# VectorE's part of a softmax: groups of four heads of one tile, with contiguous passes, in the last five full-width stretches

## The chip, the core and the metric

One core of one Trainium2 chip runs the whole program. The time is what the device takes from the start of the program to its end, in microseconds (us). The median of three runs of the kernel before is 804.98 us (804.66 to 805.05).

The core has a matrix engine (TensorE; PE in the profile, PEld its weight loads), a vector engine (VectorE, DVE), an engine for functions such as the exponential (ScalarE, ACT), a general engine (GpSimd, POOL) and SyncE (SP), which issues transfers. Matrix products land in PSUM, eight banks of 2 KB for each of 128 partitions. Everything else is kept in SBUF.

## What is computed

Two attention layers over the same 2048 x 512 input, 32 heads of width 16, mixed by a gate that is one number for each row:

```python
g = sigmoid((x * gate_w).sum(-1))
# A: full attention
scores = einsum("bhqd,bhkd->bhqk", q, k) * 16 ** -0.5
a = (softmax(scores) @ v) @ A_wo
# B: each position looks back at 8 positions, 2 apart, with a masked softmax
b = (softmax(local logits) @ v) @ B_wo
out = g * a + (1 - g) * b
```

The work is in A: 32 heads x 2048 x 2048 scores, each of which needs an exponential.

## The kernel before

**Blocks and periods.** A's scores are handled in blocks: 128 keys (a tile) x 512 queries of one head. A period is one group of 4 heads with one quarter of the queries: 16 tiles x 4 heads = 64 blocks. There are 8 groups and 4 quarters, so 32 periods; the last is cut into two halves of 256 queries, in which one block holds two tiles. The code counts periods 0 to 32, of which 31 and 32 are the halves, with 32 blocks each.

**Two ways to the exponential.** Most blocks are ScalarE's. TensorE writes the scores of three blocks, then of two, then of three, into two rings of PSUM banks (3 + 2 banks, `ring`), and ScalarE takes each set in one instruction (128 x 1536 or 128 x 1024 elements, line 1420) and writes `pT`. TensorE then multiplies `pT` with the values (`vp_all`, line 1278) into an accumulator, four heads at a time in four column strips of the array.

The others are VectorE's; `n_dve` (line 20) says how many in each period. For each such block, TensorE writes the scores into a bank `misc_ps` (`dq`, line 1332), and VectorE turns them in one instruction into 16-bit integers that read as bf16 are a coarse exponential (`p1`, line 1338, into a group's buffer `dt`). A group has `NGR` = 3 blocks. When its three are there, VectorE makes three further copies of the group, each with another constant added (`sh`, line 1357, into `pd_a`; one "pass" each), and TensorE multiplies the original and the three copies with four differently weighted copies of the values (`vp_all`, and `vd_all` for the passes; `pv` and `dpv`, lines 1367 and 1373). Their sum evens out the error of the coarse form. A group thus costs TensorE four rounds, in each of which its heads run side by side.

**Two forms of a pass.** Up to period `FLAT0` = 28 a pass is written with rows of 514 elements (`ROW`) and read in half rows (line 1361). From period 28 on it is one contiguous stretch of 3 x 512 elements on both sides (line 1363). [...]

**Buffers.** Groups from period 8 on take turns in three `dt` buffers: `dt_a` and two in `wkv`, weights that are no longer needed by then (line 507). Passes take turns in three `pd_a` buffers. PSUM has three banks besides the rings, shared by the accumulators (at most two) and by every `misc_ps`.

**B.** The local attention runs mostly on GpSimd, tile by tile, 16 tiles of 43 us; its projections use the weights `bw`. When GpSimd has made the rows of a tile (`obb`), TensorE transposes them and VectorE copies them (`fin` and `oe`, lines 1210 and 1217). GpSimd also scales A's finished accumulators (`po2a`, `po2b`, lines 1462 and 1465) except in the last three periods, where VectorE does.

**Order.** No engine chooses its order when it runs. Every piece of work is an `op` with its engine, a cost, a due time, what it depends on and which buffers it takes. `list_schedule` (line 181) walks through time and picks for each engine the piece that is next; what comes out is written to each engine's queue as it stands, and each engine works through its own in order, waiting where an input or a buffer is not ready. `sets` and `beside` (lines 447 to 471) decide beside which of ScalarE's sets a VectorE block's scores are written: at most one to a set, and by preference one of a head that the set does not have. `p1` has a due time 100 us ahead of need (`P1D`, line 123), so that it goes before the passes.

Of the kernel before, what the change touches and what calls it, by code (L numbers as in the profile page):

```python
# [9 lines left out]
ALU = mybir.AluOpType  # L10
AX = mybir.AxisListType
FP32 = mybir.dt.float32
BF16 = mybir.dt.bfloat16
# [3 lines left out]

CFG = dict(
    set_sizes=(3, 2),
    n_dve=(3, 3, 6, 6, 9, 9, 12, 12) + (12,) * 20 + (15,) + (15,) * 2 + (6, 6),  # L20
    dve_tiles=4,
    b_start=36.0,
    b_space=(43.0,) * 16,
# [7 lines left out]
DIL = 2  # L31
QW = 512
NEG = -1.0e9
FLAT0 = 28
BITS = 128.0
LN2 = 0.6931471805599453
SHIFT = 175.0
DEXP = -2.0565
NV = 4
NGR = 3  # L40
NK1 = 2
KSB = True
KPD, KPS, KPR, KP1, KP2 = 16.0, 3.5, 20.0, 44.0, 11.0
ROW = QW + 2
# [3 lines left out]
NPD = 3  # L48
NDE = 1
NDL = 3  # L50
SPREAD = (0.75, 0.88, 0.6)
STEP = 32.0
# [48 lines left out]
GFIRST = -300.0  # L101
DMAQ, DMAL = 1.0, 6.0
NPR = 3
PRE = 0.14
POOL_G, NPG = (), 1
MARGIN = {("pool", "pe"): 4.0, ("pool", "dve"): 3.0, ("pool", "act"): 3.0, ("pool", "sp"): 3.0, ("dve", "pool"): 1.5}
QD = 20.0
SM_V, PO_V = False, False
# [199 lines left out]
def kernel(  # L308
# [96 lines left out]
    def tok(tag, cap):  # L405
        name = "banks" if tag in ("misc", "acc") else tag
        if name not in res:
            res[name] = Banks(3) if name == "banks" else Res(cap)
        return Tok(res[name], tag)
# [14 lines left out]
    width = lambda pi: q_cols(pi).stop - q_cols(pi).start  # L424
    parts_of = lambda pi, t: [(t_, slice(n_ * width(pi), (n_ + 1) * width(pi))) for n_, t_ in enumerate(tiles_of(pi, t))]
    n_dve = cfg["n_dve"]
    vtiles = list(range(NT - 1, NT - 1 - NTD, -1))
    seq, first_unit, lastj = [], [], []
    nu = 0
    for pi in range(NP):  # L430
        first_unit.append(nu)
        n = n_dve[pi]
        assert n % NGR == 0 and n <= 4 * NTD
        nt_ = NT // len(tiles_of(pi, 0))
        vt_ = vtiles if nt_ == NT else [nt_ - 1, nt_ - 2]
        taken = [(t, j) for t in vt_ for j in range(4)][:n]
        rest = [(t, j) for t in range(nt_) for j in range(4) if (t, j) not in taken]
        own = []
        while rest:
            u_ = next((x for x in rest if x[1] not in lastj), rest[0])  # L440
            rest.remove(u_)
            own.append(u_)
            lastj = [lastj[-1], u_[1]] if lastj else [u_[1]]
        nu += len(own)
        seq.append((own, [taken[k_:k_ + NGR] for k_ in range(0, n, NGR)]))
    first_unit.append(nu)
    sets, beside = [], {}
    cur = []
# [53 lines left out]
    kmax_b = const.tile([128, NG], BF16, name="kmax_b")  # L502
    negk = const.tile([128, NG], FP32, name="negk")
    dt_a = const.tile([128, NDE * NGR * QW], BF16, name="dt_a")
    pd_a = const.tile([128, (NPD + NPG) * NGR * ROW], BF16, name="pd_a")
    wkv_l = wkv[:].rearrange("p c n -> p (c n)")
    dt_bufs = [dt_a[:, k_ * NGR * QW:(k_ + 1) * NGR * QW] for k_ in range(NDE)]
    dt_bufs += [wkv_l[:, k_ * NGR * QW:(k_ + 1) * NGR * QW] for k_ in range(NDL - NDE)]
    pd_bufs = [pd_a[:, k_ * NGR * ROW:(k_ + 1) * NGR * ROW].rearrange("p (q n) -> p q n", q=NGR) for k_ in range(NPD + NPG)]
    stage = pd_a[:, 0:DC * D].rearrange("p (c n) -> p c n", c=DC)  # L510
    ott2 = const.tile([128, 1, BPC, 32], BF16, name="ott2")
    g_sp = const.tile([128, NT], FP32, name="g_sp")
# [449 lines left out]
    o_gr = op("dve", 0.12, zcopy, GT + 9, deps=[a], use=[tzr])  # L962


    o_kvd, o_obt = [], []
    obt_tiles, obt_tok = {}, {}
    WP = WH // 2
    HB = D // 2
# [1 line left out]
    def b_tile(t):  # L970
# [37 lines left out]

        def qe():
            V.tensor_scalar(out=st["qb"][:], in0=st["pq"][:], scalar1=float(DH) ** -0.5, scalar2=None, op0=ALU.mult)  # L1010
        tk = tok("misc", 2)
        a = op("pe", WAVE(2), proj("pq", 0, 0), tb - 24 - QB, full=2, deps=[o_bw] + o_xt[cb], alloc=[tk, tqb], rel=rel)
        a = op("pe", WAVE(2), proj("pq", 0, 2), tb - 23.5 - QB, full=2, deps=[a], use=[tk])
        qa = op("dve", 0.61, qe, tb - 23 - QB, deps=[a], use=[tk, tqb])

        def load(key, off, hf):
# [280 lines left out]
    def pv_take(pend, tn, flush):  # L1297
        while pend:
# [7 lines left out]
                pv_run(pend[q_:min(n, q_ + 4)], tn)  # L1306
            del pend[:n]

    wkv_users = [o for o in ops if o.eng == "pe" and o.name.startswith(("kp", "vp"))]
    d_st, d_last, d_sh = {}, [None, None], []  # L1310
    d_count, d_ends, d_sg = [0, 0, 0, 0], [], []

    def d_set(pi, gi, t, j, qk_, tn):

        c_, i = periods[pi]
        late = pi >= LATE0
        key = (pi, gi)
        first = key not in d_st
        if first:
            slot = d_count[0] % NDL if late else d_count[2] % NDE  # L1320
            d_count[0] += late
            d_count[2] += not late
            d_st[key] = dict(dt=dt_bufs[slot], td=tok("dtl", NDL) if late else tok("dt", NDE), js=[], ts=[], p1=[])
        g = d_st[key]
        n_ = len(g["js"])
        g["js"].append(j)
        g["ts"].append(t)

        st = {}
        tx = tok("misc", 2)  # L1330

        def dq():
            st["x"] = misc_ps([128, QW])
            for t_, cs in parts_of(pi, t):
                mm(st["x"][:, cs], kt_all[32 * j:32 * j + 32, i, t_ * 128:(t_ + 1) * 128], qt_tiles[pi][32 * j:32 * j + 32, q_cols(pi)],
                   True, True, tile_position=(32 * j, 0))

        def p1():
            V.tensor_scalar(out=g["dt"][:, n_ * QW:(n_ + 1) * QW].bitcast(U16), in0=st["x"][:], scalar1=float(DH) ** -0.5 * BITS / LN2,
                            scalar2=(127.0 + DEXP + SHIFT * float(DH) ** -0.5 / LN2) * BITS, op0=ALU.mult, op1=ALU.add)  # L1340
        deps = [o_q[pi], o_k[i][tiles_of(pi, t)[0] // TPC]] + [o_vd[(4 * i + j, t_)] for t_ in tiles_of(pi, t)]
        if first and late and d_count[0] <= NDL:
            deps += wkv_users + d_ends[-NV * NDE:]
        a = op("pe", 0.0, dq, tn - 3.0, mode="r", js=[j], deps=deps, alloc=[tx] + ([g["td"]] if first else []),
               use=[q_tok[pi]] + ([] if first else [g["td"]]), after=[qk_, d_last[1]], ride=True, name=f"dq{pi}")
        d_last[1] = a
        o = op("dve", 0.61, p1, tn + P1D, deps=[a], use=[tx, g["td"]], after=[d_last[0]], name=f"p1_{pi}")
        d_last[0] = o
        g["p1"].append(o)
        if len(g["js"]) < NGR:  # L1350
            return
        vs = [o_vd[(4 * i + j_, t2)] for t_, j_ in zip(g["ts"], g["js"]) for t2 in tiles_of(pi, t_)]

        def on_pool(m):
            return m == NV - 1 and gi in POOL_G

        def sh(m, pb):
            def s():
                o_, i_ = pb.bitcast(U16)[:, :, 0:QW], g["dt"].bitcast(U16)
                if pi < FLAT0:  # L1360
                    i_ = _ap(i_, [list(i_.ap[0]), [QW // 2, 2 * NGR], [1, QW // 2]])
                else:
                    o_ = o_.rearrange("p q n -> p (q n)")
                (G if on_pool(m) else V).tensor_scalar(out=o_, in0=i_, scalar1=STEP * m, scalar2=None, op0=ALU.add)
            return s

        def pv(m, pb):
            def s():
                pv_mm(pi, [(t_, j_, pb[:, n1, 0:QW]) for n1, (t_, j_) in enumerate(zip(g["ts"], g["js"]))],
                      lambda t2: vd_all[:, m - 1, t2 - (NT - NTD)] if m else vp_all[:, t2])  # L1370
            return s

        def dpv(m, pb, deps, use, dl):
            b = op("pe", 0.0, pv(m, pb), dl, mode="c", js=g["js"], full=1, deps=deps + [o_t0[pi]] + vs,
                   use=[use, acc_tok[pi]], name=f"dpv{pi}")
            o_pv[pi].append(b)
            d_ends.append(b)
        dpv(0, g["dt"].rearrange("p (q n) -> p q n", q=NGR), list(g["p1"]), g["td"], tn + 4.5)
        for m in range(1, NV):
            if on_pool(m):  # L1380
                pb = pd_bufs[NPD + d_count[3] % NPG]
                d_count[3] += 1
                tp = tok("pg", NPG)
                a = op("pool", 0.0, sh(m, pb), GFIRST, deps=list(g["p1"]), alloc=[tp], use=[g["td"]], name=f"sg{pi}",
                       after=d_sg[-1:], parts=GP("one", NGR * QW))
                d_sg.append(a)
            else:
                pb = pd_bufs[d_count[1] % NPD]
                if pi >= FLAT0:
                    k0 = d_count[1] % NPD * NGR * ROW  # L1390
                    pb = pd_a[:, k0:k0 + NGR * QW].rearrange("p (q n) -> p q n", q=NGR)
                d_count[1] += 1
                tp = tok("pd", NPD)
                a = op("dve", 0.0, sh(m, pb), tn + 1.5 + SHD * (m - 1), deps=list(g["p1"]), alloc=[tp], use=[g["td"]],
                       lat=(0.065 + NGR * QW / 1920.0 if pi < FLAT0 else 0.1 + NGR * QW / 3840.0) + SH_LAT, after=d_sh[-1:],
                       parts=[(False, 0.065 + NGR * QW / 1920.0)] if pi < FLAT0 else PT(NGR * QW), name=f"sh{pi}")
                d_sh.append(a)
            dpv(m, pb, [a], tp, tn + 4.5 + SHD * m)

    pend, dwait = [], []  # L1400
# [214 lines left out]
```

## Time and profile before

| | |
|---|---|
| median of 3 runs | 804.98 us |
| profiled execution, its own time | 803.36 us |
| its span, first to last instruction | 801.6 us |
| busy: ACT / PE / DVE / POOL | 777.5 / 741.8 / 687.4 / 638.2 us |
| granted TensorE clock | 1.00 |

In the page's strips each digit is the busy share of 20 us in tenths. A group is all instructions of one line, engine and shape, with the mean time of one. Nearly all instructions are issued through helpers, so their line is 370 or 379 and the buffers' names tell them apart: `wkv<-misc_ps` and `dt_a<-misc_ps` are `p1`, `pd_a<-wkv` and `pd_a<-dt_a` are passes, `pT<-ring` is ScalarE's exponential. A view by stretches gives each engine's busy time between two times of the span. The periods are placed by ScalarE's sets: period 27 runs from about 680.4 to 704.2 us, 28 to 726.4, 29 to 748.6, 30 to 770.8, and the halves to 782.5 and 794.9.

### The profile page before, as it was taken

What the parts mean: (1) busy time and instruction counts of PE and PEld (TensorE: products, weight loads), DVE (VectorE), ACT (ScalarE), POOL (GpSimd) and SP (SyncE); (2) the same over time, 40 slices, a digit from 0 to 9 for tenths busy, and PEclk for the clock granted to TensorE, in tenths of its full rate; (3) what the DMA queues carried; (4) which work ended last, traced back from release to release, by engine and by line L of the source; (5) the groups of instructions that cost most, each with busy time, mean ns of one, the idle gap of its engine ahead of it and who ended that gap; (6) DMA issues with size and microseconds to landing.
All of it is one profiled execution on the core that took longest, in us unless ns stands there. A gap on an engine that the chain in (4) does not pass through costs nothing.

```text
span 801.6 us, 17762 instructions
## 1 busy us (share of the span) xinstructions
PE 741.8 (93%) x6806; PEld 243.6 (30%) x6864; DVE 687.4 (86%) x1105; ACT 777.5 (97%) x700; POOL 638.2 (80%) x1067
## 2 busy tenths in 40 slices
PE   8999999999999999999999999998999999889997
PEld 5333333333222222222222232232222233222333
DVE  5638787998886999999998899899998989988886
ACT  3999999999999999999999999999999999999996
POOL 4098989998999997899989999999989999960000
PEclk9999999999999999999999999999999999999999
DMA  7413071716344525235353535244524361100000
GB/s 265 125 35 106 32 166 48 174 45 145 92 106 121 143 68 151 67 103 135 84 135 98 140 90 148 79 107 119 145 63 103 126 145 41 40 8 21 1 2 28
DMA packets 58886, 77.21 MB, mean 96 GB/s; under 512 B 3744, under 2 KB 50848, under 8 KB 58800
## 3 DMA queue, kind: packets, MB, share of 16 engines
q1 hardware_dynamic: 52608, 53.91, 21.2%
q0 software_dynamic: 6048, 22.02, 14.8%
q8 instruction: 53, 0.87, 0.4%
q14 instruction: 33, 0.27, 0.1%
q10 hardware_dynamic: 144, 0.13, 0.0%
HBM read 43.78 MB, written 10.26 MB: 67 GB/s over the span
## 4 chain that ended last, share of the span: by engine, by line
ACT 49%; PE 25%; issue 21%; DVE 4%; DMA 1%; SPq 0%; ACTq 0%; DVEq 0%
ACT pT L370 48%; PE misc_ps L379 16%; PE ring L379 8%; DVE pd_a L370 1%; DMA xld<-in_A_x_dram 1%; DVE dt_a L370 1%; ACT lg L370 1%; DVE vd_all L370 1%; DVE wkv L370 0%; DVE kt_all L370 0%; PE pxt L645 0%; DVE vp_all L370 0%; DVE ssum L370 0%; DVE rr L370 0%; DVE qa L370 0%
## 5 line engine op out<-in xcount | busy, mean ns | idle before, releaser
L370 ACT ACTIVATE pT<-ring 128x1536 bf16<-128x1536 f32 (+1 forms) x677 | 769.6, 1322 | 9.2 <-PE ring L379 6.0
L379 PE MATMUL ring<-qt,kt_all 32*128 32x512 bf16 (+1 forms) x1743 | 266.2, 375 | 44.3 <-ACT pT L370 36.4
L379 PE MATMUL misc_ps<-pT,vp_all 128*17 128x512 bf16 (+2 forms) x1743 | 202.7, 377 | 0.4 <-DVE dt_a L370 0.2
L370 POOL TENSOR_TENSOR prod<-ksh,qb 128x256 f32<-128x256 bf16 x256 | 177.7, 765 | 29.6 <-DMA ksh<-kv_scr 26.8
L379 PEld LDWEIGHTS <-kt_all 32*128 32x128 bf16 x2112 | 92.0, 91 | 293.6 <-issue 284.6
L370 POOL TENSOR_TENSOR prod<-prod 128x256 f32<-128x256 f32 (+1 forms) x256 | 170.4, 680 | 5.9
L370 DVE TENSOR_SCALAR pd_a<-wkv 128x1536 uint16<-128x1536 uint16 x198 | 166.1, 866 | 2.3 <-PE misc_ps L379 1.7
L370 DVE TENSOR_SCALAR wkv<-misc_ps 128x512 uint16<-128x512 f32 x198 | 132.7, 682 | 27.2 <-PE misc_ps L379 25.6
L370 DVE TENSOR_SCALAR pd_a<-dt_a 128x1536 uint16<-128x1536 uint16 x159 | 139.1, 897 | 1.5 <-PE misc_ps L379 0.8
L379 PE MATMUL misc_ps<-pd_a,vd_all 128*17 128x512 bf16 (+1 forms) x1107 | 134.8, 375 | 0.2
L379 PE MATMUL misc_ps<-qt,kt_all 32*128 32x512 bf16 (+1 forms) x369 | 129.0, 373 | 3.4 <-DVE dt_a L370 1.8
L379 PE MATMUL misc_ps<-z 128*32 128x512 bf16 (+1 forms) x391 | 128.7, 386 | 1.6 <-DVE z L370 1.6
L370 DVE TENSOR_SCALAR dt_a<-misc_ps 128x512 uint16<-128x512 f32 x159 | 106.2, 682 | 26.5 <-PE misc_ps L379 24.9
L370 POOL TENSOR_TENSOR prod<-vsh,lg 128x256 f32<-128x256 bf16 x128 | 82.8, 763 | 0.0
L379 PEld LDWEIGHTS <-vp_all 128*17 128x17 bf16 (+1 forms) x2112 | 56.1, 88 | 86.6 <-issue 74.2
L370 POOL TENSOR_TENSOR av<-vsh,lg 128x256 f32<-128x256 bf16 x128 | 77.7, 643 | 0.0
L379 PE MATMUL misc_ps<-bw,xT 128*128 128x512 bf16 x163 | 50.6, 384 | 1.9 <-issue 1.4
L379 PEld LDWEIGHTS <-vd_all 128*17 128x17 bf16 x1107 | 36.0, 88 | 50.2 <-issue 41.8
L379 PEld LDWEIGHTS <-z 128*32 128x32 bf16 x391 | 33.9, 96 | 45.2 <-issue 25.1
L370 POOL TENSOR_TENSOR rden<-rden,g_rw 128x16 f32<-128x16 f32 x30 | 8.3, 278 | 38.9 <-DVE rden L370 38.7
L379 PEld LDWEIGHTS <-xT 128*128 128x128 bf16 x576 | 28.7, 97 | 33.4 <-issue 30.4
L379 PE MATMUL misc_ps<-wkv,vp_all 128*17 128x512 bf16 (+1 forms) x207 | 33.0, 372 | 0.0
(97 smaller groups left out, 535.2 us busy)
## 6 DMA issues: line engine op xcount, KB each, us to landing
ksh<-kv_scr SPq DMA_DIRECT2D x32, 512.0 KB
vsh<-kv_scr SPq DMA_DIRECT2D x32, 512.0 KB
av<-prod POOLq DMA_DIRECT2D x28, 512.0 KB, 6.3
av<-av POOLq DMA_DIRECT2D x14, 512.0 KB, 4.9
kv_scr<-kvs SPq DMA_DIRECT2D x16, 256.0 KB
qt<-q_scr SPq DMA_DIRECT2D x30, 128.0 KB
out_dram<-osb SPq DMA_DIRECT2D x15, 128.0 KB
xld<-in_A_x_dram SPq DMA_DIRECT2D x3, 512.0 KB
```

Source lines behind the costliest of these rows:

```text
L370: return chain_on(key, f(*a, **k))
L379: return chain(nc.tensor.matmul(out, lhsT=lhsT, rhs=rhs, start=start, stop=stop, **kw))
```

## The change

From period 27 on, a VectorE group is the four heads of one tile (`NGF` = 4) and its passes are contiguous, 4 x 512 elements. Period 27 changes form with it (`FLAT0` 28 to 27). The blocks of VectorE in periods 27 to 32 go from 12, 15, 15, 15, 6, 6 to 16, 16, 16, 16, 8, 4. The `dt` buffers of these groups lie in `bw`, B's weights, and the first three wait for the last uses of `bw`; `pd_a` is cut into three of 4 x 512. A branch that could give a pass to GpSimd (`POOL_G`) was empty and goes.

```diff
-    n_dve=(3, 3, 6, 6, 9, 9, 12, 12) + (12,) * 20 + (15,) + (15,) * 2 + (6, 6),
+    n_dve=(3, 3, 6, 6, 9, 9, 12, 12) + (12,) * 19 + (16,) * 4 + (8, 4),
...
-FLAT0 = 28
+FLAT0 = 27
...
+NGF = 4
...
-POOL_G, NPG = (), 1
...
+    group_of = lambda pi: NGR if pi < FLAT0 else NGF
...
-        assert n % NGR == 0 and n <= 4 * NTD
+        gr = group_of(pi)
+        assert n % gr == 0 and n <= 4 * NTD
...
-        seq.append((own, [taken[k_:k_ + NGR] for k_ in range(0, n, NGR)]))
+        seq.append((own, [taken[k_:k_ + gr] for k_ in range(0, n, gr)]))
...
-    pd_a = const.tile([128, (NPD + NPG) * NGR * ROW], BF16, name="pd_a")
+    pd_a = const.tile([128, NPD * max(NGR * ROW, NGF * QW)], BF16, name="pd_a")
...
+        bw_users.append(a)
...
+    bw_l = bw[:].rearrange("p c n -> p (c n)")
...
-            slot = d_count[0] % NDL if late else d_count[2] % NDE
-            d_count[0] += late
+            slot = d_count[3] % NDL if flat else d_count[0] % NDL if late else d_count[2] % NDE
+            d_count[3] += flat
+            d_count[0] += late and not flat
...
-            d_st[key] = dict(dt=dt_bufs[slot], td=tok("dtl", NDL) if late else tok("dt", NDE), js=[], ts=[], p1=[])
+            d_st[key] = dict(dt=bw_l[:, slot * gr * QW:(slot + 1) * gr * QW] if flat else dt_bufs[slot],
+                             td=tok("dtf", NDL) if flat else tok("dtl", NDL) if late else tok("dt", NDE), js=[], ts=[], p1=[])
...
-        if first and late and d_count[0] <= NDL:
+        if first and flat and d_count[3] <= NDL:
+            deps += bw_users
+        elif first and late and d_count[0] <= NDL:
             deps += wkv_users + d_ends[-NV * NDE:]
...
-        if len(g["js"]) < NGR:
+        if len(g["js"]) < gr:
             return
...
-                if pi < FLAT0:
+                if not flat:
...
-                if pi >= FLAT0:
-                    k0 = d_count[1] % NPD * NGR * ROW
-                    pb = pd_a[:, k0:k0 + NGR * QW].rearrange("p (q n) -> p q n", q=NGR)
...
+            if flat:
+                k0 = d_count[1] % NPD * gr * QW
+                pb = pd_a[:, k0:k0 + gr * QW].rearrange("p (q n) -> p q n", q=gr)
```

More of the change, by code (lines that the diff above doesn't have):

```diff
@@ L508 @@
     dt_bufs += [wkv_l[:, k_ * NGR * QW:(k_ + 1) * NGR * QW] for k_ in range(NDL - NDE)]
-    pd_bufs = [pd_a[:, k_ * NGR * ROW:(k_ + 1) * NGR * ROW].rearrange("p (q n) -> p q n", q=NGR) for k_ in range(NPD + NPG)]
+    pd_bufs = [pd_a[:, k_ * NGR * ROW:(k_ + 1) * NGR * ROW].rearrange("p (q n) -> p q n", q=NGR) for k_ in range(NPD)]
     stage = pd_a[:, 0:DC * D].rearrange("p (c n) -> p c n", c=DC)
@@ L962 @@
     o_gr = op("dve", 0.12, zcopy, GT + 9, deps=[a], use=[tzr])
-    o_kvd, o_obt = [], []
+    o_kvd, o_obt, bw_users = [], [], []
     obt_tiles, obt_tok = {}, {}
@@ L1013, in b_tile @@
         a = op("pe", WAVE(2), proj("pq", 0, 2), tb - 23.5 - QB, full=2, deps=[a], use=[tk])
+        bw_users.append(a)
         qa = op("dve", 0.61, qe, tb - 23 - QB, deps=[a], use=[tk, tqb])
@@ L1307, in pv_take @@
             del pend[:n]
+    bw_l = bw[:].rearrange("p c n -> p (c n)")
     wkv_users = [o for o in ops if o.eng == "pe" and o.name.startswith(("kp", "vp"))]
     d_st, d_last, d_sh = {}, [None, None], []
-    d_count, d_ends, d_sg = [0, 0, 0, 0], [], []
+    d_count, d_ends = [0, 0, 0, 0], []
     def d_set(pi, gi, t, j, qk_, tn):
@@ L1316, in d_set @@
         late = pi >= LATE0
+        flat, gr = pi >= FLAT0, group_of(pi)
         key = (pi, gi)
@@ L1349, in d_set @@
         g["p1"].append(o)
-        if len(g["js"]) < NGR:
+        if len(g["js"]) < gr:
             return
         vs = [o_vd[(4 * i + j_, t2)] for t_, j_ in zip(g["ts"], g["js"]) for t2 in tiles_of(pi, t_)]
-        def on_pool(m):
-            return m == NV - 1 and gi in POOL_G
         def sh(m, pb):
@@ L1363, in s @@
                     o_ = o_.rearrange("p q n -> p (q n)")
-                (G if on_pool(m) else V).tensor_scalar(out=o_, in0=i_, scalar1=STEP * m, scalar2=None, op0=ALU.add)
+                V.tensor_scalar(out=o_, in0=i_, scalar1=STEP * m, scalar2=None, op0=ALU.add)
             return s
@@ L1377, in dpv @@
             d_ends.append(b)
-        dpv(0, g["dt"].rearrange("p (q n) -> p q n", q=NGR), list(g["p1"]), g["td"], tn + 4.5)
+        dpv(0, g["dt"].rearrange("p (q n) -> p q n", q=gr), list(g["p1"]), g["td"], tn + 4.5)
         for m in range(1, NV):
[L1380 to L1388, printed above, removed]
-                if pi >= FLAT0:
-                    k0 = d_count[1] % NPD * NGR * ROW
-                    pb = pd_a[:, k0:k0 + NGR * QW].rearrange("p (q n) -> p q n", q=NGR)
[L1392 to L1397, printed above, removed]
+            pb = pd_bufs[d_count[1] % NPD]
+            if flat:
+                k0 = d_count[1] % NPD * gr * QW
+                pb = pd_a[:, k0:k0 + gr * QW].rearrange("p (q n) -> p q n", q=gr)
+            d_count[1] += 1
+            tp = tok("pd", NPD)
+            a = op("dve", 0.0, sh(m, pb), tn + 1.5 + SHD * (m - 1), deps=list(g["p1"]), alloc=[tp], use=[g["td"]],
+                   lat=(0.065 + NGR * QW / 1920.0 if not flat else 0.1 + gr * QW / 3840.0) + SH_LAT, after=d_sh[-1:],
+                   parts=[(False, 0.065 + NGR * QW / 1920.0)] if not flat else PT(gr * QW), name=f"sh{pi}")
+            d_sh.append(a)
             dpv(m, pb, [a], tp, tn + 4.5 + SHD * m)
```

## The prediction

> **What bounds the kernel now.** I read the page first: the busy shares, the strips by time and the chain that ended last.
>
> ```profile
> PE 741.8 (93%) x6806; PEld 243.6 (30%) x6864; DVE 687.4 (86%) x1105; ACT 777.5 (97%) x700; POOL 638.2 (80%) x1067
> ACT  3999999999999999999999999999999999999996
> POOL 4098989998999997899989999999989999960000
> PEclk9999999999999999999999999999999999999999
> ACT 49%; PE 25%; issue 21%; DVE 4%; DMA 1%; SPq 0%; ACTq 0%; DVEq 0%
> ```
>
> ScalarE is busy in every slice but the first and the last, and has the largest part of the chain; the clock is at full speed. GpSimd has work until about 716 us, so the new form of a pass meets it in period 27 and not much later. Next, the view by stretches, cut at the periods that the change touches, with two stretches from the middle.
>
> ```profile
> 680.40:704.20 23.80, 20.99 (x199) 6.91 (x198) 20.33 (x30) 23.80 (x23) 23.22 (x38) 1.00 0.12 37
> 704.20:726.40 22.20, 19.63 (x195) 6.03 (x188) 19.13 (x36) 22.20 (x21) 10.97 (x16) 1.00 0.05 14
> 726.40:748.60 22.20, 20.52 (x196) 6.25 (x190) 18.31 (x34) 22.20 (x21) 1.03 (x2) 1.00 0.04 13
> 748.60:770.80 22.20, 21.81 (x184) 6.57 (x183) 18.83 (x33) 22.12 (x21) 0.85 (x2) 1.00 0.00 1
> 770.80:782.50 11.70, 10.85 (x174) 4.99 (x174) 9.98 (x20) 11.63 (x11) 0.00 (x0) 1.00 0.01 4
> 782.50:794.90 12.40, 10.73 (x187) 5.33 (x187) 9.60 (x19) 12.38 (x12) 0.00 (x0) 1.00 0.07 23
> 320.00:345.00 25.00, 23.59 (x201) 6.93 (x203) 24.51 (x36) 25.00 (x23) 21.62 (x37) 1.00 0.25 59
> 345.00:370.00 25.00, 22.82 (x201) 6.28 (x196) 24.55 (x38) 25.00 (x24) 24.15 (x41) 1.00 0.63 160
> ```
>
> The columns are the stretch, its length, then PE, PEld, DVE, ACT and POOL busy. ScalarE never pauses in the six stretches that change (0.08 us in 748.6 to 770.8, 0.07 and 0.02 in the halves), while VectorE is at 85, 86, 82, 85, 85 and 77%. The last two rows matter most for what follows: there VectorE is busy for 49.06 of 50 us, 98%, and ScalarE still does not lose a hundredth. So a block moved from ScalarE to VectorE is worth its time on ScalarE as long as VectorE has the room, and room up to about 98% has been seen to be usable.
>
> **ScalarE's gain.** VectorE's blocks in periods 27 to 32 go from 12+15+15+15+6+6 = 69 to 16+16+16+16+8+4 = 76. ScalarE loses seven blocks, 1691 to 1684. From the timeline of ScalarE:
>
> ```profile
> 687.43 107.45 ACT L370 ACTIVATE pT<-ring 128x1536 bf16<-128x1536 f32 x95
> 797.87 0.59 ACT L370 CAST osb<-misc_ps 128x512 bf16<-128x512 f32 x1 [2.99 <-PE misc_ps L379]
> ```
>
> These 95 sets are 47 pairs of three and two blocks, and a last one of one: 236 blocks, 0.4553 us each. Seven are 3.19 us. What follows ScalarE's last exponential (794.88 to 801.6) holds no group's passes that must be later than now, and again begins with a set of one block (1684 is 336 pairs, then 3 and 1), so I leave it as it is, within 0.4 us on either side.
>
> **VectorE, period by period.** Its prices in period 27, and after GpSimd has finished:
>
> ```profile
> L370 DVE TENSOR_SCALAR pd_a<-wkv 128x1536 uint16<-128x1536 uint16 x9 | 8.3, 948 | 0.2 <-PE misc_ps L379 0.2
> L370 DVE TENSOR_SCALAR wkv<-misc_ps 128x512 uint16<-128x512 f32 x10 | 6.7, 681 | 2.4 <-PE misc_ps L379 2.3
> ...
> L370 DVE TENSOR_SCALAR wkv<-misc_ps 128x512 uint16<-128x512 f32 x24 | 16.3, 687 | 4.0 <-PE misc_ps L379 3.9
> L370 DVE TENSOR_SCALAR pd_a<-wkv 128x1536 uint16<-128x1536 uint16 x21 | 11.1, 556 | 0.3 <-PE misc_ps L379 0.2
> ```
>
> A strided pass takes 0.948 us, a contiguous one of the same 1536 elements 0.556 us. One of 2048 elements is not there as a pass, but seven instructions of the same kind, contiguous 16-bit elements from SBUF to SBUF, are in the part where the keys are prepared, all with GpSimd at work:
>
> ```profile
> L370 DVE TENSOR_SCALAR kt_all<-kt_all,rowc,negk 128x2048 bf16<-128x2048 bf16 x7 | 6.4, 917 | 0.1
> L370 DVE TENSOR_SCALAR kt_all<-kt_all,rowc,negk x7: 715/823/1399, 37.0 to 174.0; 128x2048 bf16<-128x2048 bf16 x7
> ...
> 119.57 1.20 POOL L370 TENSOR_TENSOR prod<-ksh,qb 128x256 f32<-128x256 bf16 x1
> 120.73 1.42 POOL L370 TENSOR_TENSOR obb<-av 128x256 bf16<-128x256 f32 x2
> 122.11 0.67 POOL L370 TENSOR_TENSOR prod<-ksh,qb 128x256 f32<-128x256 bf16 x1
> ```
>
> The second row gives the least, the middle and the longest: 0.715, 0.823 and 1.399 us, with a mean of 0.917. So a 2048-wide pass lies between 0.556 (the narrower one, alone) and 0.917 (beside GpSimd). Beside GpSimd I take 0.917, the row that is the same in every way; alone I take 0.715, the least of the seven, in which GpSimd was least in the way.
>
> - Period 27: four more p1 (4 x 0.681 = 2.72), twelve passes at 0.917 for twelve at 0.948 (-0.37): 20.33 becomes 22.68. ScalarE now needs 48 x 0.4553 = 21.85. VectorE is over by 0.83 us.
> - Period 28: one p1 (0.69), twelve passes at 0.715 for fifteen at 0.556 (8.58 for 8.34, +0.24), and about 1.0 for five of them that still meet GpSimd: 19.13 becomes 21.06 of 21.85. With 0.83 carried over it is level.
> - Periods 29 and 30: 18.31 becomes 19.24 and 18.83 becomes 19.76, of 21.85 each.
> - First half: two p1 and six wider passes (1.37 + 0.95): 9.98 becomes 12.3, where ScalarE needs 24 x 0.4553 = 10.93. Over by 1.4.
> - Second half: two p1 and three passes fewer, the other three wider (-1.37 - 1.19): 9.60 becomes 7.0 of 12.75. What the first half left over fits in.
>
> Together 102.0 us of VectorE in 111.1 of ScalarE, 92%. In two places demand is over supply by 0.83 and 1.4 us. p1 goes ahead of the passes, and three groups may be open, so what is late are one or two passes and their products, whose accumulator closes later; ScalarE is not delayed by that until a p1 is late, its bank is kept, and TensorE stands before a score that wants this bank, with ScalarE's next set queued behind it. The loss to ScalarE is thus between 0 and 2.2 us. The rows at 98% lie nearest to the case and show no loss, so I take 0.4.
>
> **TensorE.** In periods 28 to 30 each has 4 groups x 4 rounds instead of 5 x 4, the second half 4 rounds fewer; a round starts 0.22 us after the one before, whether it has three strips or four:
>
> ```profile
> 703.98 0.39 PE L379 MATMUL misc_ps<-pd_a,vd_all 128*17 128x512 bf16 x3
> 704.20 0.39 PE L379 MATMUL misc_ps<-pd_a,vd_all 128*17 128x512 bf16 x3
> ...
> PE ring L379 <- ACT pT L370: 5.9, 14, 1.0
> ...
> PE misc_ps L379 <- DVE wkv L370: 0.2, 1, 0.2
> ```
>
> Some 12 rounds, 2.6 us, go, and seven scores come that mostly run beside ScalarE's in a free row strip. I count this as nothing: TensorE waits for ScalarE before the ring (5.9 us after 704), and after 600 us it waits for VectorE's p1 for 0.2 us in all.
>
> **New waits and GpSimd.** The first three groups wait for the last use of `bw`, and the first new passes overlap two old buffers each.
>
> ```profile
> L379 PE MATMUL misc_ps<-bw,xT x10: 379/379/390, 613.1 to 624.1; 128*128 128x512 bf16 x10
> ...
> 678.14 1.81 DVE L370 TENSOR_SCALAR pd_a<-dt_a 128x1536 uint16<-128x1536 uint16 x2
> ...
> 684.05 0.95 DVE L370 TENSOR_SCALAR pd_a<-wkv 128x1536 uint16<-128x1536 uint16 x1
> ...
> 714.12 1.76 POOL L370 TENSOR_TENSOR obb<-av 128x256 bf16<-128x256 f32 x2
> ...
> 724.61 0.42 DVE L370 COPY obt<-misc_ps 128x512 bf16<-128x512 bf16 x1 [0.22 <-PE misc_ps L1215]
> ```
>
> `bw` is free at 624, 56 us ahead. The old period's last passes end at 679.95, and a first pass of period 27, which now needs four p1, cannot come before 684: four us for the products of the old ones. Both cost nothing; were the cover gone, each us would stop TensorE's queue, the scores for ScalarE in it, for as long. GpSimd loses about 0.53 us to a 2048-wide instruction (1.20 against 0.67 above): 12 x 0.53 = 6.4 us, so its last `obb` ends near 722 instead of 715.9. Its user on TensorE's queue ran at about 724, and what comes of it is an output tile whose products run after 760. Nothing, if the order leaves those eight us or moves along. No transfer is moved past another; those that follow a period's end come 2 us earlier.
>
> [...]
>
> **The sum.** Against the profiled execution: 803.36 - 3.19 + 0.4 = 800.6 (span 798.8). The median shown lies 1.62 above that execution, so 802.2.
>
> **Rivals.**
> [...]
> 2. *VectorE becomes the bound in all the long periods (slower).* Place: periods 27 to 30. It decides from a shortfall of 1.2 us a period, 4.8 in all, where 3.19 is given back and 1.6 more lost: 806.6. In period 28 all but the passes is 19.13 - 8.34 + 0.69 = 11.48 us, so a pass would have to take (21.85 + 1.2 - 11.48)/12 = 0.96 us without GpSimd. The dearest mean in the trace is 0.917, with GpSimd. But p1 is also served more slowly if it stands behind longer passes, at a period's change, when two accumulators leave one bank; that I cannot price from a row. 807.2, say 2.2 us over.
> 3. *The change does not do what it says:* the blocks go to VectorE but TensorE's fixed order, made with other prices, keeps ScalarE waiting for just what it gained: 804.98 within 0.5.
>
> **Chances and range.** Forecast (a gain of over 1.6 us): 0.69. Rivals 1 and 3: 0.12 and 0.05. Rival 2: 0.14. A measurement of this kernel can tell 0.2%, 1.6 us, from no change; so faster 0.69, same 0.17, slower 0.14. The low end is the gain without any loss (801.8), less 0.4 in the tail and 0.2 for the spread of the runs: 801.2; the high end takes in rival 1 and half of rival 3 and leaves rival 2 out: 805.0. The forecast's own range is 801.2 to 803.3.
>
> **What would show it.** ScalarE: 674 sets, some 3.2 us less busy, and still no more than 0.5 us of idle time between 680 us and its end. VectorE: 48 + 6 + 3 passes of 128x2048, near 0.9 us before 722 and near 0.7 after; busy 95 to 100% in period 27. GpSimd's last long work ends near 722. TensorE: no wait for VectorE of over 1 us. The prediction is wrong if ScalarE waits for the ring in period 27 or in the first half, if a 2048-wide pass alone takes over 0.9 us, or if the end after ScalarE's last set grows.

## The result and the profile after

The changed kernel has a median of 800.0 us in six runs (799.5 to 803.18). In the same series the kernel before has 804.59, a little lower than in the three runs shown ahead of the prediction. The ratio is 0.9963, with a 95% interval of 0.9950 to 0.9976: 3.0 us less, 802.0 on the scale of the 804.98 from which the prediction was made. Forecast were 802.2 and a gain. The ratio is not the quotient of the two medians: that is 0.9943, or 4.6 us, which lies outside the interval and is more than all seven blocks can be worth (3.19 us). Why the two differ so much here is not shown. In the second series, below, the ratio gives 3.4 us and the medians 2.9, so this text goes by the ratios.

The profiled execution took 803.18 us, with a span of 800.3. It is one of the two slowest of the six, and why is part of the story. Its page, the lines that answer to those shown of before:

```profile
PE 741.5 (93%) x6817; PEld 241.9 (30%) x6876; DVE 692.6 (87%) x1100; ACT 774.5 (97%) x697; POOL 644.3 (81%) x1067
ACT  3999999999999999999999999999999999999996
POOL 4098989899999997899989899999989999991000
ACT 50%; PE 23%; issue 22%; DVE 4%; DMA 1%; SPq 0%; ACTq 0%; DVEq 0%
```

ScalarE is still the bound, with three instructions and 3.0 us fewer. GpSimd's strip ends one slice later. The view by stretches, cut where ScalarE, by its count of blocks, passes from period to period (27 to 30, then the two halves; columns as before):

```profile
681.00:703.10 22.10, 20.23 (x202) 6.24 (x194) 20.17 (x31) 22.10 (x22) 20.55 (x27) 1.00 0.12 39
703.10:726.20 23.10, 21.66 (x181) 5.92 (x180) 19.07 (x30) 22.02 (x21) 19.47 (x27) 0.93 0.02 7
726.20:748.00 21.80, 20.30 (x202) 6.32 (x199) 19.67 (x34) 21.80 (x20) 1.16 (x2) 1.00 0.07 20
748.00:769.80 21.80, 20.49 (x202) 6.75 (x200) 20.70 (x35) 21.80 (x20) 1.16 (x2) 1.00 0.01 2
769.80:780.70 10.90, 10.35 (x139) 4.20 (x140) 8.89 (x16) 10.90 (x11) 0.00 (x0) 1.00 0.01 2
780.70:793.40 12.70, 12.22 (x224) 5.98 (x223) 10.24 (x20) 12.70 (x12) 0.00 (x0) 1.00 0.01 2
```

VectorE carries 76 blocks in these stretches and is at 81 to 95%; ScalarE is full in all but one. In the second row it stands for 1.08 us, and there the granted clock is 0.93. The timeline of ScalarE shows 0.81 us of it as one stop, and the fine view by stretches shows what goes before it:

```profile
687.18 24.11 ACT L370 ACTIVATE pT<-ring 128x1024 bf16<-128x1024 f32 x21
712.10 81.31 ACT L370 ACTIVATE pT<-ring 128x1536 bf16<-128x1536 f32 x72 [0.81 <-PE ring L379]
```

```profile
706.00:707.00 1.00, 0.78 (x13) 0.36 (x10) 1.00 (x2) 0.95 (x2) 1.00 (x2) 1.00 0.00 0
707.00:708.00 1.00, 0.77 (x8) 0.25 (x7) 0.77 (x2) 1.00 (x2) 1.00 (x3) 1.00 0.03 8
708.00:709.00 1.00, 1.00 (x9) 0.26 (x8) 1.00 (x4) 1.00 (x2) 0.70 (x2) 0.68 0.00 0
709.00:710.00 1.00, 1.00 (x6) 0.12 (x4) 0.50 (x1) 1.00 (x1) 0.91 (x2) 0.50 0.00 0
710.00:711.00 1.00, 1.00 (x9) 0.12 (x5) 0.37 (x1) 0.85 (x2) 1.00 (x3) 0.50 0.00 0
711.00:712.00 1.00, 1.00 (x12) 0.18 (x11) 0.92 (x2) 0.29 (x1) 1.00 (x2) 0.62 0.06 16
```

The third column from the end is the clock. At the change from period 27 to 28 TensorE is busy for 1.55 of two us, then its clock is halved for 3.4 us, the scores come more slowly and ScalarE runs out. (Half of 3.4 us is 0.002 of 800: an execution with one such fall has a mean clock of 0.998, and the two slowest of the six have just that.)

VectorE's passes beside GpSimd and after it, and GpSimd's last long work:

```profile
L370 DVE TENSOR_SCALAR pd_a<-bw 128x2048 uint16<-128x2048 uint16 x16 | 14.3, 908 | 0.1
...
L370 DVE TENSOR_SCALAR pd_a<-bw 128x2048 uint16<-128x2048 uint16 x41 | 27.0, 680 | 0.1
...
703.54 1.13 DVE L370 TENSOR_SCALAR pd_a<-bw 128x2048 uint16<-128x2048 uint16 x1
...
705.79 1.13 DVE L370 TENSOR_SCALAR pd_a<-bw 128x2048 uint16<-128x2048 uint16 x1
...
723.97 1.89 DVE L370 TENSOR_SCALAR pd_a<-bw 128x2048 uint16<-128x2048 uint16 x3
...
721.56 1.41 POOL L370 TENSOR_TENSOR obb<-av 128x256 bf16<-128x256 f32 x2
```

The first group is from 680 to 720 us, the second from 724 on: 0.908 and 0.680 us a pass. The last two passes of period 27 run at 703.5 and 705.8, after ScalarE has gone on to period 28 at 703.1. Of the twelve passes of period 28 four have started by 720 us, three follow at 723.97, and five are left when ScalarE goes on to period 29 at 726.2.

### The profile page after: what moved, and what is told of

It is laid out like the page before. It is cut to its first block, busy times and chain, and to the rows that moved or that the text cites. A ratio compares the mean times of both kernels' runs of the same rounds, so it can differ in the third digit from the quotient of the medians.

```text
span 800.3 us, 17773 instructions
## 1 busy us (share of the span) xinstructions
PE 741.5 (93%) x6817; PEld 241.9 (30%) x6876; DVE 692.6 (87%) x1100; ACT 774.5 (97%) x697; POOL 644.3 (81%) x1067
## 4 chain that ended last, share of the span: by engine, by line
ACT 50%; PE 23%; issue 22%; DVE 4%; DMA 1%; SPq 0%; ACTq 0%; DVEq 0%
ACT pT L370 49%; PE misc_ps L379 15%; PE ring L379 7%; DVE pd_a L370 1%; DMA xld<-in_A_x_dram 1%; DVE dt_a L370 1%; ACT lg L370 1%; DVE vd_all L370 1%; DVE wkv L370 0%; DVE kt_all L370 0%; PE pxt L647 0%; DVE vp_all L370 0%; DVE ssum L370 0%; DVE rr L370 0%; DVE osb L370 0%
## 5 line engine op out<-in xcount | busy, mean ns | idle before, releaser
L379 PE MATMUL misc_ps<-pT,vp_all 128*17 128x512 bf16 (+3 forms) x1736 | 201.9, 377 | 0.3 <-DVE dt_a L370 0.2
L370 DVE TENSOR_SCALAR pd_a<-wkv 128x1536 uint16<-128x1536 uint16 x150 | 137.2, 940 | 1.0 <-PE misc_ps L379 0.6
L379 PE MATMUL misc_ps<-pd_a,vd_all 128*17 128x512 bf16 (+1 forms) x1128 | 131.1, 375 | 0.5 <-DVE pd_a L370 0.4
L379 PE MATMUL misc_ps<-z 128*32 128x512 bf16 x382 | 127.9, 388 | 1.6 <-DVE z L370 1.6
L370 DVE TENSOR_SCALAR pd_a<-dt_a 128x1536 uint16<-128x1536 uint16 x138 | 126.5, 939 | 0.6
L370 DVE TENSOR_SCALAR wkv<-misc_ps 128x512 uint16<-128x512 f32 x150 | 100.1, 681 | 18.5 <-PE misc_ps L379 17.6
L370 DVE TENSOR_SCALAR dt_a<-misc_ps 128x512 uint16<-128x512 f32 x138 | 92.1, 682 | 21.0 <-PE misc_ps L379 19.6
L370 DVE TENSOR_SCALAR bw<-misc_ps 128x512 uint16<-128x512 f32 x76 | 50.8, 684 | 10.8 <-PE misc_ps L379 10.2
L370 DVE TENSOR_SCALAR pd_a<-bw 128x2048 uint16<-128x2048 uint16 x57 | 41.2, 744 | 0.1
```

The source lines that it names most:

```text
L370: return chain_on(key, f(*a, **k))
L379: return chain(nc.tensor.matmul(out, lhsT=lhsT, rhs=rhs, start=start, stop=stop, **kw))
```

## The experiments

Two things were open: what the load itself costs (VectorE's demand, and passes of 0.908 us beside GpSimd against 0.680 after it; the expectations call this the port, a name of the author's, and no run shows that a port is the cause) and whether the stop at 711 us belongs to the change. Twelve kernels were run, in three sets, each set beside the kernel before on one chip. All differ from the changed kernel by the edits shown.

### The changed kernel again

No edit.

> The changed kernel once more, beside the others. Theory (port and clock): seven blocks fewer free 3.2 us of ScalarE; the contiguous passes of period 27 and the start of 28 take 0.9 us beside GpSimd instead of 0.68, TensorE stands before them between 704 and 708 us, its granted clock falls to half for some 3 us and ScalarE waits about 0.8 us. Ratio to the kernel before 0.9963, the stop near 711 us seen again. Rival (chance): the fall of the clock was one run's; it isn't seen again and the ratio is nearer 0.9960, the whole 3.2 us.

Ratio 0.9958 (0.9942 to 0.9974), median 800.68. ScalarE in its profiled execution:

```profile
687.40 104.90 ACT L370 ACTIVATE pT<-ring 128x1024 bf16<-128x1024 f32 x93
795.47 0.58 ACT L370 CAST osb<-misc_ps 128x512 bf16<-128x512 f32 x1 [3.17 <-PE misc_ps L379]
```

There is no stop. The 93 sets hold 231 blocks, 0.4541 us each, where the kernel before had 236 at 0.4553; the profile ahead of this one needed 106.23 us for the same 93 sets, so the stop near 711 us, behind the fall of the clock at 708, cost it 1.3 us. In this execution the clock falls for 3.4 us at 551 us instead, in a period that the change leaves as it was, and ScalarE stands for some 1.2 us there. The rival (chance) holds for the place; that the clock falls at all is common to both kernels, for ten of the eighteen executions of the kernel before in this set have a mean clock of 0.998 or less.

### Period 27 put back

```diff
-    n_dve=(3, 3, 6, 6, 9, 9, 12, 12) + (12,) * 19 + (16,) * 4 + (8, 4),
+    n_dve=(3, 3, 6, 6, 9, 9, 12, 12) + (12,) * 20 + (16,) * 3 + (8, 4),
-FLAT0 = 27
+FLAT0 = 28
```

> Period 27 as before (12 blocks in groups of three, strided passes), the rest as changed: 72 blocks on VectorE, three more than before. Port and clock: no contiguous pass meets much of GpSimd's work, no fall of the clock, ScalarE idle under 0.3 us after 680; gain 3 x 0.455 = 1.4 us, ratio 0.9983. Rival (load): groups of four with 16 blocks are too much wherever they are; ScalarE is stopped for 0.5 us or more in periods 28 to 30 and the ratio is 0.999 or more.

Ratio 0.9990 (0.9977 to 1.0002). ScalarE waits 0.2 us in all after 600 us in the profiled execution, so the load is not too much in periods 28 to 30. The time is 0.6 us above the expected, within the interval; seven of twelve executions have a mean clock of 0.997 or less, more than the changed kernel has. By the two ratios, four blocks in period 27 are worth 2.6 us against the run above, where 1.8 were due; the intervals are wide enough for either, and the clocks differ too.

### GpSimd's work cut

The kernel leaves out most of the products of B's last two tiles, and with them their output.

```diff
+                hb, hn = (32, 2) if t >= NT - 2 else (HB, HB // DH)
                 if hf == 0:
-                    o_ = av[:, wp + w_, c0:c0 + HB]
+                    o_ = av[:, wp + w_, c0:c0 + hb]
...
-                cs = slice(c0, c0 + HB)
+                cs = slice(c0, c0 + (32 if t >= NT - 2 else HB))
```

> The changed kernel with the order of every engine kept, but GpSimd's multiplications and sums of B's last two tiles take 32 of 256 columns (the rest of these products is left out, so the output of the last two tiles' B part is not the reference's). Port and clock: passes of period 27 near 0.72 us, no fall of the clock, ScalarE idle under 0.2 us between 680 us and its end, 0.5 to 1 us faster than the changed kernel. Rival (order): the stop near 711 us comes from the fixed order and stays, time as the changed kernel within 0.3 us.

Ratio 0.9955 (0.9939 to 0.9971), median 800.21 against 800.68.

```profile
L370 DVE TENSOR_SCALAR pd_a<-bw 128x2048 uint16<-128x2048 uint16 x19 | 13.0, 708 | 0.1
...
686.47 104.75 ACT L370 ACTIVATE pT<-ring 128x1024 bf16<-128x1024 f32 x93
```

The passes of 676 to 723 us fall from 0.908 us to 0.708, as expected, and ScalarE's 93 sets take 104.75 us instead of 104.90. What GpSimd's work adds to a pass is real for VectorE, 0.2 us, and in the time there is next to nothing of it: 0.15 us of ScalarE. This half of the theory falls for this kernel.

### The planner told the dearer pass

```diff
-                   ... if not flat else PT(gr * QW), name=f"sh{pi}")
+                   ... if not flat else [(True, 0.1 + gr * QW / 3840.0 + (0.25 if pi <= FLAT0 + 1 else 0.0))], name=f"sh{pi}")
```

(The same 0.25 goes into the latency.)

> The changed kernel, but the planner counts a pass of periods 27 and 28 at 0.88 us instead of 0.63, near the 0.9 us measured beside GpSimd. Port and clock: TensorE's order no longer asks for a pass before it is there, no fall of the clock, 0.3 to 1 us faster than the changed kernel. Rival (order doesn't matter): the same stop at the same place, no difference over 0.3 us; or the planner itself now delays scores and ScalarE waits elsewhere, slower by up to 1 us.

Ratio 0.9954 (0.9938 to 0.9970), median 800.33. No stop near 711 us, but the changed kernel did not show one either in this set. The 0.35 us between the two cannot be told from no change; nothing is shown.

### The new form from period 26 on

```diff
-    n_dve=(3, 3, 6, 6, 9, 9, 12, 12) + (12,) * 19 + (16,) * 4 + (8, 4),
+    n_dve=(3, 3, 6, 6, 9, 9, 12, 12) + (12,) * 18 + (16,) * 5 + (8, 4),
-FLAT0 = 27
+FLAT0 = 26
```

> The new form from period 26 on, with 16 blocks there too: 80 blocks on VectorE, 4 more than the changed kernel. By the prediction's sum VectorE's demand in period 26 is 21.65 + 2.72 - 0.4 = 24.0 us for 21.85 of ScalarE, 0.8 over again in 27, level in 28, room from 29 on. Theory (late passes cost nothing while three groups may be open): ScalarE still idles under 0.5 us after 640, another 1.8 us gained, ratio to the kernel before 0.9937. Rival (98% is the limit): the 2.8 us that are over come back as waits of ScalarE for the ring between 660 and 725, ratio 0.9965 or more.

Ratio 1.0028 (1.0009 to 1.0046): slower than before.

```profile
784.43 6.88 ACT L370 ACTIVATE pT<-ring 128x1536 bf16<-128x1536 f32 x6 [0.34 <-PE misc_ps L379]
799.81 0.59 ACT L370 CAST osb<-misc_ps 128x512 bf16<-128x512 f32 x1 [8.49 <-PE misc_ps L379]
```

ScalarE's exponentials end at 791.3, and then it stands for 8.5 us before its last copy out of PSUM (`osb`): 12.2 us from its last exponential to the end of the span, where the changed kernel has 6.9. Neither theory had this. The demand that is over in 26 and 27 does not come back as waits of ScalarE where it arises; VectorE's last blocks come at the end instead. In the plan, pieces of VectorE and GpSimd that are marked `True`, the contiguous passes among them, take turns at one `port` (in `list_schedule`); that is the plan's assumption, and no run shows such a port. Whether the planner puts the last blocks late because of it is what the next run asks.

### The same, with a planner that does not count `port`

The edit of the variant before (five periods of 16 blocks, the new form from 26 on), and:

```diff
-                   ... if not flat else PT(gr * QW), name=f"sh{pi}")
+                   ... if not flat else [(False, 0.1 + gr * QW / 3840.0)], name=f"sh{pi}")
```

> The new form with 16 blocks from period 26 on, but the planner no longer counts a pass as holding the shared port, so it believes VectorE to be on time and writes another order. Theory (with the planner's port the order put VectorE's last blocks late, and that, not the demand, made the end long): the stretch behind ScalarE's last exponential falls from 12.2 us to under 8, ratio 0.995 or less, better than both kernels. Rival (demand: VectorE really is behind, the plan only says so): the end stays long or ScalarE waits between 660 and 730, ratio 0.998 to 1.004.

Ratio 1.0016 (1.0007 to 1.0024). Three of the waits after 600 us (first the engine that waits, then the one it waits for; us in all, how often, the longest):

```profile
PE misc_ps L379 <- DVE pd_a L370: 4.7, 10, 0.9
ACT pT L370 <- PE misc_ps L379: 3.9, 7, 0.7
ACT pT L370 <- PE ring L379: 1.6, 4, 1.0
```

The end is short again (6.6 us), as the theory said, and ScalarE now waits for 5.5 us instead, as the rival said. In this execution the clock fell at 661 us, and 1.1 us of the wait come right behind that; but seven of the eleven executions have a mean clock of 1.000 and still take 803.92 to 805.13 us. Four blocks more are 1.8 us for ScalarE, and VectorE does not have the room for them beside GpSimd, whichever way the order is written: its passes take 0.948 us there on average and its p1 0.675, 57 of the 62 us from 660 to 722 for these two alone.

```profile
L370 DVE TENSOR_SCALAR pd_a<-bw 128x2048 uint16<-128x2048 uint16 x31 | 29.0, 948 | 0.1
L370 DVE TENSOR_SCALAR bw<-misc_ps 128x512 uint16<-128x512 f32 x43 | 28.2, 675 | 2.3 <-PE misc_ps L379 2.1
```

### Eight blocks in the second half too

```diff
-    ... + (16,) * 4 + (8, 4),
+    ... + (16,) * 4 + (8, 8),
```

> 8 blocks in the second half too: 80 blocks. Theory: VectorE's demand in the last half is 7.0 + 2.7 + 2.1 = 11.8 us for 10.9 of ScalarE, after a first half that is over as well; there is nothing behind it to take up late passes, so what is late is the end. ScalarE ends 1.8 us earlier than in the changed kernel, but the stretch after its last exponential grows from 6.9 to 8 or 9 us: ratio 0.995 to 0.997, no better than the changed kernel. Rival (the late passes still fit): the stretch stays below 7.2 us and the ratio is 0.994.

Ratio 1.0001 (0.9992 to 1.0010).

```profile
685.70 103.06 ACT L370 ACTIVATE pT<-ring 128x1024 bf16<-128x1024 f32 x91
797.61 0.59 ACT L370 CAST osb<-misc_ps 128x512 bf16<-128x512 f32 x1 [8.85 <-PE misc_ps L379]
```

ScalarE ends 1.84 us earlier, counted from 0.3 us after the last small exponential of B, just as expected. The stretch behind it grows from 6.9 to 12.5 us, more than the 8 to 9 expected: the last p1 ends at 789.5 and four passes follow at 792.1.

### Four and eight in the halves

```diff
-    ... + (16,) * 4 + (8, 4),
+    ... + (16,) * 4 + (4, 8),
```

> The changed kernel with 4 and 8 blocks in the halves instead of 8 and 4: as many in all, the same seven taken from ScalarE. Theory (the end must have room on VectorE): ScalarE ends as early as in the changed kernel, within 0.5 us, but the stretch behind it grows from 6.9 us to 10 to 13, as with 8 and 8: ratio 0.9995 to 1.003. Rival (only the sum of both halves counts): the stretch stays under 7.5 us and the ratio is 0.996.

Ratio 0.9988 (0.9971 to 1.0005).

```profile
779.90 13.24 ACT L370 ACTIVATE pT<-ring 128x1536 bf16<-128x1536 f32 x12 [0.26 <-ACT pT L370]
797.96 0.58 ACT L370 CAST osb<-misc_ps 128x512 bf16<-128x512 f32 x1 [4.82 <-PE misc_ps L379]
```

The same seven blocks are off ScalarE, which ends at 793.14; behind it are 8.6 us instead of 6.9. The direction is the theory's, the size is not (10 to 13 were expected). By the ratios 2 of the changed kernel's 3 us are given back. The longer end is 1.7 of them in the profile; six of the twelve executions also have a mean clock of 0.997 or less, and how much of the rest is the clock's is not shown. How the last blocks are shared between the halves is a good part of the change.

### Period 27 in the new form with its old 12 blocks

```diff
-    ... (12,) * 19 + (16,) * 4 + (8, 4),
+    ... (12,) * 20 + (16,) * 3 + (8, 4),
```

> Period 27 in the new form, but with its old 12 blocks (three groups of four): 72 blocks, as in the run in which period 27 was put back. VectorE saves 12 x 0.947 - 9 x 0.9 = 3.3 us in period 27. Theory (form alone is worth nothing, since ScalarE is the bound): ratio as that run's, 0.998 to 0.999, ScalarE idle under 0.3 us. Rival (the form itself helps, by fewer rounds and passes): 0.5 us or more faster than that run.

Ratio 0.9996 (0.9986 to 1.0006): not the 0.998 of the theory's better end, with nine of ten executions at a mean clock of 0.995 to 0.997. The tenth, at 1.000, took 800.69 us. The profile shows the same picture as the changed kernel's first one, and deeper:

```profile
706.00:708.00 2.00, 0.84 (x11) 0.32 (x11) 1.79 (x4) 2.00 (x3) 2.00 (x4) 1.00 0.01 4
708.00:710.00 2.00, 1.82 (x13) 0.60 (x10) 1.94 (x4) 2.00 (x3) 1.92 (x4) 0.64 0.00 0
710.00:712.00 2.00, 2.00 (x12) 0.38 (x13) 0.68 (x3) 0.74 (x2) 2.00 (x4) 0.51 0.00 0
```

TensorE has still less to do at the change of periods, 0.84 of 2 us; the clock falls, and ScalarE is busy for 0.74 of the two us after 710.

### The same, with more filling

Where the planner counts too few rounds of TensorE in 2.3 us, it has it multiply zeros (`z`). Here it asks for more rounds from 675 us of its plan on: 101 full-width products of zeros after 675 us instead of 82.

The edit of the variant before (12 blocks in period 27), and:

```diff
-            lack = ROWS_MIN - o.full - sum(n for _, n in self.recent)
+            lack = (8.0 if t > 675.0 else ROWS_MIN) - o.full - sum(n for _, n in self.recent)
...
-        lack = ROWS_IDLE - sum(n for tr, n in self.recent if tr > t - ROWS_SPAN)
+        lack = (10.0 if t > 675.0 else ROWS_IDLE) - sum(n for tr, n in self.recent if tr > t - ROWS_SPAN)
```

> Period 27 in the new form with 12 blocks, and the same extra filling. Without it nine of ten executions had a mean clock of 0.995 to 0.997 and the ratio was 0.9996. Theory (the hole and the clock): clock 0.999 to 1.000, no wait of over 0.5 us of ScalarE near 711, 1.4 us below the kernel before: ratio 0.998. Rival (12 contiguous blocks are worth nothing for another reason): ratio stays at 0.9996, clock as without filling.

Ratio 0.9981 (0.9971 to 0.9991), ten of twelve executions at 0.999 or 1.000. ScalarE's part runs through without a stop:

```profile
687.47 105.68 ACT L370 ACTIVATE pT<-ring 128x1536 bf16<-128x1536 f32 x93
```

So the 1.2 us that the 12 blocks lacked look like the clock's, and products of zeros bring them back. The two intervals just overlap, and the edit also gives TensorE a new order.

### The changed kernel with more filling

The same two lines, with nothing else changed.

> The changed kernel, with more filling products of zeros on TensorE from 675 us of the plan on (the planner asks for 8 and 10 rounds in 2.3 us instead of 6.5 and 8). Theory (a hole in TensorE's work at the change of periods halves its clock in some executions): no execution's mean clock under 0.9985 for a reason behind 675 us, the median 0 to 0.7 us below the changed kernel's 800.7, ratio to the kernel before 0.995 to 0.996. Rival (the fall has another cause): the clocks spread as before, same median; or the filling delays scores and ScalarE waits, 0.5 to 1.5 us slower.

Ratio 0.9966 (0.9953 to 0.9979), median 800.92, clocks of 0.998 to 1.000 as without. With 16 blocks the filling brings nothing that can be told; the theory's gain is not there, and two of the five executions are at 0.998, under the 0.9985 that it named.

### The load without the form

```diff
-    ... (12,) * 19 + (16,) * 4 + (8, 4),
+    ... (12,) * 19 + (15,) + (16,) * 3 + (8, 4),
-FLAT0 = 27
+FLAT0 = 28
```

> Period 27 with 15 blocks in groups of three and strided passes (the rest as changed): the load without the new form, 75 blocks. VectorE's demand in period 27 is 20.33 + 3 x 0.681 + 3 x 0.948 = 25.2 us for 22.3 of ScalarE, 2.9 over. Theory (form makes the load possible): passes run late into period 28, and either ScalarE waits 1 to 2.5 us between 690 and 725 or, if late passes cost nothing, none; in the first case 0 to 1 us slower than with 12 blocks there, in the second 1.4 us faster (ratio 0.9965).

Ratio 1.0013 (0.9999 to 1.0028), all but one execution at a mean clock of 0.988 to 0.995.

```profile
690.00:700.00 10.00, 8.97 (x93) 2.93 (x92) 10.00 (x15) 10.00 (x10) 10.00 (x17) 1.00 0.01 2
700.00:710.00 10.00, 8.87 (x89) 2.82 (x87) 9.97 (x13) 10.00 (x10) 10.00 (x17) 1.00 0.00 1
710.00:720.00 10.00, 9.01 (x52) 1.89 (x53) 8.02 (x13) 7.91 (x7) 5.88 (x9) 0.61 0.01 2
720.00:730.00 10.00, 9.64 (x60) 1.72 (x57) 6.05 (x11) 6.31 (x6) 0.00 (x0) 0.54 0.00 0
```

VectorE is full from 690 to 710, 19.97 of 20 us. ScalarE does not notice then; from 712 on TensorE's clock is at half for 17 us, five times 3.41, and ScalarE stands for 5.8 of the 20 us from 710. This execution is the slowest of the ten. What goes before the fall is one contiguous pass, the first of period 28:

```profile
708.37 2.90 DVE L370 TENSOR_SCALAR pd_a<-bw 128x2048 uint16<-128x2048 uint16 x1
...
711.33 0.39 PE L379 MATMUL misc_ps<-pd_a,vd_all 128*17 128x512 bf16 x4 [0.76 <-DVE pd_a L370]
```

It takes 2.9 us; GpSimd is busy for all 20 us from 690 to 710 and for 5.88 of the ten after; and TensorE stands for 0.76 us before its product. By the ratios of this kernel and of period 27 put back, three blocks more in the strided form cost 1.9 us, where four more in the contiguous form saved 2.6, each with more than 1 us on either side. The loss seems to come by way of the clock: the one execution at 0.998 took 801.03 us, no more than the fastest with 12 blocks there (801.16). That fits the theory, in which late work stops ScalarE, but the profile has the contiguous pass of 2.9 us, beside a busy GpSimd, in it too, and only one execution was profiled.

## Why the prediction was right, point by point

- **ScalarE's gain: right.** 674 sets, and 0.4541 us a block in the execution without a stop against 0.4553. The lowest spans in the second series, without and with the change, are 800.7 and 797.4 us, 3.3 apart for the 3.19 forecast. The variants give doses of the same: four blocks more in the second half take 1.84 us off ScalarE, and three with the clock held (period 27 with 12 blocks and more filling) are worth 1.5 us of time where 1.4 were due.
- **The price of a pass: right.** 0.908 us beside GpSimd for 0.917; alone 0.680 for 0.715, the nearest row being a little dear.
- **VectorE's demand: right in sum, only in part in place.** In all six stretches VectorE is busy for 98.7 us, where 102.0 were summed; the cheaper pass after 724 us makes about 1.4 of the difference. The two halves hold 19.1 us, as summed (19.3), and three passes and two p1 of the first run in the second, as its 1.4 us over said, though VectorE is busy for only 8.89 of 10.90 us in the first. Period 27 was to be over by 0.83 us and busy for 95 to 100%. It does leave two passes over (2.3 us), but VectorE is busy for 20.17 of 22.10 us, 91%, and waits for scores in most of the rest. Period 28 was to be level and leaves five over; 29 leaves three and 30 one. That late passes cost ScalarE nothing thus held for more of them than the one or two expected.
- **The loss of 0.4 us: not confirmed, and its mechanism was not seen.** Gains of 3.0 and 3.4 us, each with about 1 us on either side, fit a loss of 0.4 and a loss of nothing; that 802.2 lies so near 802.0 is in part luck. The loss was to come from late p1, kept banks and a standing TensorE. TensorE waited for VectorE's passes for 0.4 us in all after 680, and in the execution without a stop ScalarE waited for TensorE for 0.2 us in all from 600 to 795. In the other it lost 1.3 us behind a fall of the clock. The prediction had no term for that: it took the clock as given at 1.00 from one execution. Nor is it shown to be a cost of the change: three of the changed kernel's twelve executions have a mean clock of 0.998 or less, and 38 of the 80 of the kernel before that ran beside the experiments.
- **TensorE's rounds:** by the prediction's own terms 16 go (three periods with four fewer, and four in the second half), not 12; both were counted as nothing, and after 680 us TensorE's longest wait for VectorE's passes is 0.2 us. Whether fewer rounds make a fall at the change of periods more likely is open: the clock fell there in one of the changed kernel's two profiled executions and in that of the variant with 12 contiguous blocks, and it held in the kernel before, where TensorE had less to do than in the changed kernel.
- **Rival 1 (chance 0.12, and part of the high end of the range):** it stood for contiguous passes dearer than the 0.917 us of the seven rows by a price that no run shows. What the runs showed is a mean of 0.908 us beside GpSimd, and 0.948 in the run from period 26 on without `port`; cutting GpSimd's work moved ScalarE by 0.15 us. Single passes are dearer: the two of 1.13 us above, beside GpSimd's instructions of 0.6 to 1.0 us, and one of 2.9 us in the strided variant, against 0.680 alone. What makes them so long is not shown. As a cost of this change it does not matter.
- **Rival 2, VectorE as the bound:** not here, but one step away. 16 blocks in period 26 as well end slower than before, and 15 in strided form in period 27 give the whole gain back. The prediction's rule that 98% is usable and that late passes cost nothing holds only while something later can take them up: in the halves, 4 and 8 give most of the gain back at the end, 8 and 8 all of it.
- **Nothing at the end:** right. 6.9 us behind ScalarE's last exponential, 6.7 before. The runs show that this was not safe: it is 8.6 to 12.5 in three variants.
- **GpSimd** ended its last `obb` at 722.97, forecast 722; the passes of period 27 begin at 684.70, and `bw` and the old passes made no wait.

## What to carry to other kernels

In this kernel, moving work to an engine that is off the critical path paid at the full price of the relieved engine, as long as the receiver's demand stayed under the time that the bound engine leaves, with a stretch behind that had room for what was late; the last stretch has none. Shares of busy time do not tell when that ends: sum the demand in each stretch, at the prices measured beside the same neighbours. And one profile does not tell about TensorE's clock: read it over several executions of both kernels before a stop is put down to a change.

## What the runs showed of the hardware

The clock's falls were not expected. In five profiled executions, at 120 to 124 us (the kernel with 4 and 8), 551 to 554 (the changed kernel again), 661 to 664 (from period 26 on, no port), 708 to 712 (the changed kernel) and 709 to 712 (12 blocks in period 27), each fall, added up from the granted clock in stretches of half a us, is 3.41 or 3.42 us at half rate. In a sixth, with 15 strided blocks, it is 17.07 us on end, five times as long. Why the changed kernel shows a fall at 708 us in one profiled execution and at 551 in the other is not shown, nor whether some amount of work prevents it. In the 3.4 us ahead of the fall TensorE was busy for 2.74 us in the changed kernel, the most of the six profiles, and at the same change of periods it was busy for 2.01 of 3.4 in the kernel before, whose clock held:

```profile
704.90:708.30 3.40, 2.74 (x29) 1.12 (x26) 3.17 (x6) 3.35 (x4) 3.40 (x6) 1.00 0.01 2
...
704.60:708.00 3.40, 2.01 (x24) 0.71 (x23) 2.67 (x6) 3.40 (x5) 2.68 (x6) 1.00 0.01 2
```

The first row is of the changed kernel, the second of the kernel before. TensorE's busy share alone does not say when the clock falls.
